# Moving the weights of a float32r kernel to other byte distances from the operands that stream past them

## The chip, the cores and the metric

The kernel runs on one core of a Trainium2 chip. The metric is the device time in microseconds (us) of one launch. Three runs of the kernel before gave 824.92, 824.91 and 824.10 us, median 824.91 us.

## The reference

One attention block feeds two feed-forward layers. All is float32, with 4 batches, 8 heads, 576 positions and head width 64.

```python
attn = softmax(mask(q @ k.T / 8)) @ v        # mask: blocks of 64 positions, block-causal
x = attn.transpose(0, 2, 1, 3).reshape(2304, 512)
h = x @ w_in                                 # 512 -> 2048
g = max(h, 0) + log1p(exp(-abs(h)))
x = g @ w_out                                # 2048 -> 512
h = x @ w_in2                                # 512 -> 1024
s = h * softmax(h)                           # over the 1024
ln = (s - mean(s)) / sqrt(var(s) + 1e-6) * g_ln
out = ln @ w_out2                            # 1024 -> 512
```

## The kernel before

**Numbers in two parts.** The feed-forward products are made from float32r operands. Every operand is split in a high part (a float32r copy) and a low part (the rest), and a product is three matmuls: high by high, high by low and low by high. So each product's stationary operand (128 x 128, called the weights below) is loaded for every matmul, and 256 or 512 columns of the moving operand stream past it.

**Layer 1** runs over 9 chunks of 256 tokens (`NCH`, `CT`), and in each over 8 pairs of blocks of 128 features (`Pair`, line 572). `Pair.a` (line 614) makes one block's `h` in 12 matmuls into the PSUM tile `hp`: weights `w1t[f]`, moving `xt` (the attention's output, high and low). ACT and DVE make `g` and split it into `gh` and `gl` (lines 623 to 642). `Pair.b` (line 647) adds the block to the output in 12 matmuls into `acc` (or `R` for chunk 1): weights `w2t[f]`, moving `gh` or `gl`. Chunks leave through DRAM (`x2s`). There are 1728 matmuls of 256 columns in `a` and 1728 in `b`.

**Layer 2** runs over 18 groups of 128 tokens (`Tok`, line 780). `Tok.a` (line 829): 24 matmuls of 512 columns into `h`; the weights are the tokens (`xh` and `xl`, which lie in `w1t[4]` and `w1t[5]`), the moving operand is `u1`. DVE and ACT make the softmax and the normalised rows `e`, PE transposes them (`tr`, line 891, float32, through `ident`) into `tp`, ACT and DVE split them into `lh` (line 900) and `ll` (line 905). `Tok.bm` (line 910): 24 matmuls of 512 columns into `op`; the weights are `lh` and `ll`, the moving operand is the second weight matrix, which lies in `w1t[6]` to `w1t[13]`. The last group makes its 24 as 48 of 256 columns.

**Where the tiles lie.** A pool's tiles stand one behind the other in each SBUF partition, in the order of their first use, with sizes rounded to 32 bytes. On the left stand the pools `w` (w1_4 to w1_15, w2_0 to w2_15, ident, gcol), `l1` (t, gh, gl, stg with 2 buffers each of 2048 bytes; 21 small tiles of 32 bytes), `xt` (3 buffers of 8192 bytes) and `wx` (w1_0 to w1_3), whose room `p2` (xr, e, ob of layer 2) takes later. On the right, against the upper end, stand the attention's pools and later `u1`. The program of the kernel before has these start addresses in bytes:

| tile | start | used as |
|---|---|---|
| w1_4 ... w1_15 | 16512 + 4096 each | weights of `Pair.a`; tokens, second matrix and `lh` in layer 2 |
| w2_0 ... w2_15 | 65664 + 4096 each | weights of `Pair.b` |
| ident | 131200 | moving operand of the transposes |
| gh, gl | 135840, 137888, 139936, 141984 | moving operand of `Pair.b` |
| xt | 148800, 156992, 165184 | moving operand of `Pair.a`; the first also `ll` in layer 2 |
| w1_0 ... w1_3 | 173376 + 4096 each | weights of `Pair.a` |
| e0, e1 | 177472, 181568 | weights of the transposes of layer 2 |
| u1 | 190432, 206816 | moving operand of `Tok.a` |

Inside a tile all steps between the blocks that one matmul reads are multiples of 512 bytes, so the distance "start of the weights minus start of the moving operand", taken modulo 512, is the same for all matmuls of one kind.

**Order.** All tasks are listed with dependencies, durations and ranks; a planner (`Plan.run`, line 89) puts them in an order once, while the program is built, and engines run their queues in that order. Waits between engines come from the tiles' regions that instructions read and write. `ln_hi` before waits for the last use of `w1t[14]` or `w1t[15]` (`w1_free`, line 763), and `t_q` (line 778), which opens the PSUM pool of `tp` and `op`, for the last matmul of layer 1, for the last readers of the first `xt` buffer, and for the last attention parts.

Of the kernel before, what the change touches and what calls it, by code (L numbers as in the profile page):

```python
# [10 lines left out]
F32 = mybir.dt.float32  # L11
F32R = mybir.dt.float32r
# [26 lines left out]
NCH = NT // CT  # L39
# [12 lines left out]
class Plan:  # L52
# [8 lines left out]
    def add(self, eng, dur, rank, fn, deps=(), lat=None):  # L61
        t = _Task()
        t.key = key_of(fn)

        t.alts = dict(eng) if isinstance(eng, dict) else {eng: dur}
        name, i = t.group = self.group
        t.local = rank
        t.rank = rank + RANK[name][0] + RANK[name][1] * i + OFF.get(t.key, 0.0) + OFF.get(t.key + "@" + name, 0.0)
        t.eng, t.fn, t.n, t.done = None if len(t.alts) > 1 else eng, fn, len(self.tasks), False
        t.lat = (self.LAT + (120.0 if eng == "PE" else 0.0)) if lat is None else lat  # L70
        t.users, t.left, t.ready = [], 0, 0.0
        for d in deps:
            if d is not None:
                d.users.append(t)
                t.left += 1
        self.tasks.append(t)
        return t
# [5 lines left out]
    def chain(self, eng, rank, steps, deps):  # L83
        for dur, fn in steps:
            t = self.add(dur if isinstance(dur, dict) else eng, dur, rank, fn, deps)
            deps = [t]
        return t
# [83 lines left out]
def key_of(fn):  # L171
    while isinstance(fn, partial):
        fn = fn.func
    return ".".join(fn.__qualname__.split(".")[-2:])


def act_ns(n):
    return 70.0 + 0.833 * n


def dve_ns(n, per=1.04):
    return 70.0 + per * n
# [6 lines left out]
def dma_ns(nbytes, n=1):  # L189
    return max(50.0 + nbytes / 360.0, 550.0 * n)  # L190
# [3 lines left out]
def body(ctx: ExitStack, tc: tile.TileContext, qk, qkA, vP, vA, w1, w2, u1, u2, gln, out):  # L194
    nc = tc.nc
    PE, ACT, DVE, POOL, SP = nc.tensor, nc.scalar, nc.vector, nc.gpsimd, nc.sync
    plan = Plan()
    XTB, LAG = 3, 2
    add, chain = plan.add, plan.chain
# [13 lines left out]
    def at_of(lst, i):  # L213
        return lst[i] if 0 <= i < len(lst) else None
# [4 lines left out]
    def pool(name, side, **kw):  # L219
        return tc.tile_pool(name=name, bufs=1, side=side, reuse_waits="tile", **kw)  # L220
# [3 lines left out]
    pw = left.enter_context(pool("w", "left"))  # L224
    pl1 = left.enter_context(pool("l1", "left"))
    pxt = left.enter_context(pool("xt", "left"))
# [3 lines left out]
    state = {}  # L230


    w1t = [(px if f < 4 else pw).tile([128, 2, 512], F32R, name=f"w1_{f}") for f in range(16)]
    w2t = [pw.tile([128, 2, 512], F32R, name=f"w2_{f}") for f in range(16)]
    ident = pw.tile([128, 128], F32, name="ident")
    gcol = pw.tile([128, 8], F32, name="gcol")
    acc = qsh.tile([128, 2, 512], F32, name="acc")
    hps = [qsh.tile([128, 2, CT], F32, name=f"hp{i}") for i in range(2)]

# [58 lines left out]
    xt = {}  # L298

    def xt_of(c):  # L300
        if c not in xt:
            xt[c] = pxt.tile([128, 2, 4, CT], F32R, tag="xt", name="xt", bufs=XTB)
        return xt[c]


# [6 lines left out]
    def xfree(c):  # L312

        return [t for u in pairs if u.c == c - XTB for t in (u.t_a0, u.t_a1)]
# [255 lines left out]
    xparts = {}  # L570
# [94 lines left out]
    stored, evacs = {}, {}  # L665
# [27 lines left out]
    def open_u():  # L693
        right[0].close()
        right[0] = ExitStack()
        pu1 = right[0].enter_context(pool("u1", "right"))
        state["qh2"] = right[0].enter_context(pool("qh2", "right", space=PSUM))
        state["u1"] = [pu1.tile([128, 4, DF2], F32R, name=f"u1{i}") for i in range(2)]
        state["cv"] = [(pu1.tile([128, 512, 2], I32, name="raw_u"), pu1.tile([128, 512], I32, name="a_u"))]
        SP.dma_start(out=gcol, in_=gln)  # L700

    def open_2():
# [10 lines left out]
    def open_q():  # L713
        psl.close()
        state["qtr"] = left.enter_context(pool("qtr", "left", space=PSUM))
        state["ll"] = xt_of(NCH).rearrange("p a b c -> p (a b c)")

    NR, NCA = 3, 4
    t_open = add("POOL", 500, 0.0, open_a, ())
# [1 line left out]
    pairs, unitsA, unitsC = [], [], []  # L721
# [9 lines left out]
    def w_of(t, i):  # L731
        return lambda: t[:, i]
# [7 lines left out]
    for kind, f in todo:  # L740
        src, t, done = (w1[f], w1t[f], w1ready) if kind == "w1" else (w2[f * 128:f * 128 + 128, :], w2t[f], w2ready)
        p = Piece(src, w_of(t, 0), w_of(t, 1))
# [8 lines left out]
    t_b = add("DVE", 200, 0, open_b, [u.t_xl for u in unitsA] + [x for p in pieces for x in (p.t_lo, p.t_hi)] + evacs[1])  # L751
# [5 lines left out]
    t_u = add("SP", 1, 0, open_u, [x for u in unitsC for x in u.t_x])  # L757
    upieces, u1d, u2d = [], [], []

    def u1_of(i, f):  # L760
        return lambda: state["u1"][i][:, :, f * 128:f * 128 + 128]

    def w1_free(f):
        return [(pairs[8 * (NCH - 1) + f // 2].t_a0, pairs[8 * (NCH - 1) + f // 2].t_a1)[f % 2]]

    for f in range(8):
        p = Piece(u1[f], u1_of(0, f), u1_of(1, f))
# [4 lines left out]
    for f in range(8):  # L772
        p = Piece(u2[f * 128:f * 128 + 128, :], w_of(w1t[6 + f], 0), w_of(w1t[6 + f], 1), gcol[:, f:f + 1])
# [1 line left out]
        plan.at_group("U2", f)  # L775
        p.plan(upieces, 0.0, conv_u, 3 if f > 2 else n + 1, 3 if f > 2 else n + 1, [t_u, t_2], w1_free(6 + f))
        u2d.append(p.t_lo)
    t_q = add("PE", 1, 0, open_q, evacs[NCH - 1] + [pairs[-1].t_b1, t_u] + xfree(NCH) + xparts[NCH - 1])

    class Tok:  # L780
        def __init__(self, t):
# [2 lines left out]
        def plan(self, prev):  # L784
            t = self.t
            rank = 0.0
            plan.at_group("Tok", t)
            p1, p2, p3 = (at_of(prev, len(prev) - k) for k in (1, 2, 3))
            o1 = (lambda *names: [getattr(p1, x) for x in names] if p1 else [])
            o2 = (lambda *names: [getattr(p2, x) for x in names] if p2 else [])  # L790
            o3 = (lambda *names: [getattr(p3, x) for x in names] if p3 else [])
            self.t_load = add("SP", dma_ns(262144), rank - 4, self.load,
                              [t_2] + stored[t // 2] + o2("t_xl", "t_xh") + o1("t_load"), DMA_LAT)
            self.t_xh = add({"ACT": 520, "DVE": 335}, None, rank, self.x_hi, [self.t_load] + o2("t_a") + (w1_free(4 + t) if t < 2 else []))
            self.t_xl = add("DVE", 610, rank, self.x_lo, [self.t_xh])
            self.t_a = add("PE", 5600, rank + 1.9, self.a, [self.t_xl] + u1d + o2("t_u") + o1("t_a"))
            t_m = add("DVE", dve_ns(1024), rank, self.max, [self.t_a])
            t_e = add("ACT", 1090, rank, self.exp, [t_m] + o2("t_tr") + ([x.t_bits for x in upieces[-3:]] if t < 2 else []))
            self.t_u = add("DVE", dve_ns(1024), rank, self.mul, [t_e])
            t_c = chain("DVE", rank, ((600, partial(self.stats, 0)), (600, partial(self.stats, 1)), (110, self.aggr),  # L800
                                      (600, self.center)), [self.t_u])
            t_s = chain("DVE", rank, [(75, partial(self.small1, i)) for i in range(4)], [t_c])
            t_s = add("ACT", 335, rank, self.logexp, [t_s])
            self.t_s = chain("DVE", rank, [(75, partial(self.small2, i)) for i in range(3)], [t_s] + o3("t_ob"))
            self.t_tr = add("PE", 870, rank + .5, self.tr, [t_c, t_q] + o1("t_ll", "t_tr"))
            self.t_lh = add("ACT", 2 * act_ns(512), rank, self.ln_hi, [self.t_tr] + o2("t_b") + (w1_free(14 + t) if t < 2 else []))
            self.t_ll = add("DVE", 2 * dve_ns(512), rank, self.ln_lo, [self.t_lh] + [t_q])

            w = DM // 2 if t == NT // 128 - 1 else DM
            for c in range(0, DM, w):  # L810
                cols = slice(c, c + w)
                self.t_b = add("PE", 5600 * w / DM, rank + 1, partial(self.bm, cols), [self.t_ll] + u2d + o2("t_ob") + (o1("t_b") if c == 0 else [self.t_b] + o1("t_ob")))
                self.t_ob = add("ACT", act_ns(w) + 90, rank, partial(self.o_evac, cols), [self.t_b, self.t_s] + o2("t_st"))
                self.t_st = add("SP", dma_ns(512 * w), rank, partial(self.store, cols), [self.t_ob], DMA_LAT)
            prev.append(self)
# [82 lines left out]
                self.tp.append(tp)  # L898

        def ln_hi(self):  # L900
            self.lh = w1t[14 + self.t % 2].rearrange("p a (k t) -> p (a k) t", k=4)
            for g in range(2):
                ACT.activation(self.lh[:, 4 * g:4 * g + 4, :], self.tp[g], AF.Copy)

        def ln_lo(self):
            self.ll = state["ll"][:, 1024 * (self.t % 2):1024 * (self.t % 2) + 1024].rearrange("p (k t) -> p k t", k=8)
            for g in range(2):
                DVE.tensor_sub(self.ll[:, 4 * g:4 * g + 4, :], self.tp[g], self.lh[:, 4 * g:4 * g + 4, :])

# [91 lines left out]
```

## Time and profile before

| | |
|---|---|
| median of 3 runs | 824.91 us |
| the profiled execution's own time | 823.77 us |
| its span, first to last instruction | 822.0 us |
| granted TensorE clock, mean | 0.996 |
| PE, DVE, ACT busy | 97%, 66%, 48% |

The profile is one execution, so 1.77 us of its time lie around the span, and it is 1.14 us under the median. Matmuls are pipelined: a matmul's record is longer than its turn on the array, and records overlap. What a matmul costs in a full stream is the distance from its start to the next one's start, called the pitch here; it is read from the starts in the timeline, not from the mean durations.

### The profile page before, as it was taken

Reading aid. Unit: us, or ns where it says so; the run is one execution under the profiler, and the core shown is the slowest. Engines: PE = TensorE matmul, PEld = TensorE weight load, DVE = VectorE, ACT = ScalarE, POOL = GpSimd, SP = SyncE. Lnnn points to the kernel's source line nnn. Section 1 sums busy time; section 2 is a strip of 40 time slices with the busy share of each in tenths; the row PEclk is TensorE's granted clock in tenths of the full one; section 3 lists DMA queues with packets and bytes.
Section 4 is the critical chain, followed back from the end, with each engine's and each line's share of the span. In section 5 each row is a group of like instructions: output and inputs, shape, how many; then the busy total and the mean of one; then the engine's idle time right before and its main releaser. Section 6 shows DMA issues by size and latency. Waiting matters only on the chain.

```text
span 822.0 us, 14229 instructions
## 1 busy us (share of the span) xinstructions
PE 798.6 (97%) x5656; PEld 689.0 (84%) x5656; DVE 546.3 (66%) x1273; ACT 391.9 (48%) x863; POOL 0.7 (0%) x6
## 2 busy tenths in 40 slices
PE   6689999999999999999999999999999999999998
PEld 4478999999888888888888889999998888888887
DVE  6999999565565656655556653777949486766661
ACT  5666765554555555455454543646623232322232
POOL 0000000000000000000000000000000000000000
PEclk9899999999999999999999999999999999999999
DMA  5544451202121112112111100326301111110001
GB/s 180 198 159 156 167 177 56 83 31 75 48 66 41 41 41 66 41 55 77 41 41 56 44 1 26 104 83 201 116 27 52 50 36 45 52 38 27 26 26 51
DMA packets 31201, 59.63 MB, mean 73 GB/s; under 512 B 2848, under 2 KB 14368, under 8 KB 31136
## 3 DMA queue, kind: packets, MB, share of 16 engines
q1 hardware_dynamic: 31136, 58.74, 22.1%
q8 instruction: 44, 0.72, 0.4%
q14 instruction: 21, 0.17, 0.1%
HBM read 49.29 MB, written 9.44 MB: 71 GB/s over the span
## 4 chain that ended last, share of the span: by engine, by line
PE 86%; DVE 7%; DMA 3%; ACT 2%; issue 1%; SPq 0%; ACTq 0%; DVEq 0%
PE hp L203 21%; PE acc L203 21%; PE h L203 12%; PE op L203 12%; PE S L203 6%; PE O L203 5%; PE T L430 4%; DMA raw<-in_w_dram 3%; PE R L203 2%; PE tp L897 2%; DVE a L278 1%; PE r L203 1%; DVE a L274 1%; DVE mA L521 1%; DVE w L288 1%
## 5 line engine op out<-in xcount | busy, mean ns | idle before, releaser
L203 PE MATMUL hp<-xt,w 128*128 128x256 f32 x1728 | 220.1, 282 | 1.5 <-DVE t L634 1.5
L203 PEld LDWEIGHTS hp<-xt,w 128*128 128x128 f32 x1728 | 207.3, 189 | 5.5 <-issue 3.4
L203 PE MATMUL acc<-gh,w 128*128 128x256 f32 x1024 | 203.2, 287 | 0.0
L203 PEld LDWEIGHTS acc<-gh,w 128*128 128x128 f32 x1024 | 163.1, 188 | 18.8 <-issue 18.4
L203 PE MATMUL acc<-gl,w 128*128 128x256 f32 x512 | 143.4, 280 | 1.1 <-DVE gl L642 1.1
L203 PE MATMUL h<-u,w 128*128 128x512 f32 x432 | 103.5, 396 | 0.0
L203 PEld LDWEIGHTS acc<-gl,w 128*128 128x128 f32 x512 | 96.4, 188 | 1.7 <-DVE gl L642 1.7
L203 PEld LDWEIGHTS h<-u,w 128*128 128x128 f32 x432 | 80.7, 188 | 19.1
L203 PE MATMUL op<-w,w 128*128 128x512 f32 (+1 forms) x304 | 91.6, 385 | 0.0
L625 ACT ACTIVATE t<-hp 128x512 f32<-128x512 f32 x72 | 42.9, 596 | 82.8 <-PE hp L203 77.8
L209 ACT ACTIVATE ps<-T 128x512 f32<-128x512 f32 (+1 forms) x77 | 42.7, 555 | 77.1 <-PE T L430 62.3
L634 DVE SCALAR_TENSOR_TENSOR t<-hp,t 128x512 f32<-128x512 f32 x72 | 49.4, 686 | 28.7 <-ACT t L631 28.2
L203 PEld LDWEIGHTS op<-w,w 128*128 128x128 f32 x304 | 55.0, 188 | 10.6
L203 PE MATMUL op<-w,xt 128*128 128x512 f32 (+1 forms) x152 | 58.0, 382 | 0.0
L409 ACT ACTIVATE eC<-S,mC 128x384 f32<-128x384 f32 (+2 forms) x80 | 51.8, 654 | 11.5 <-DVE mC L403 11.4
L399 DVE TENSOR_REDUCE mC<-S 128x2 f32<-128x768 f32 (+2 forms) x48 | 46.9, 976 | 8.5 <-PE S L203 7.8
L203 PE MATMUL S<-qkC 64*128 64x384 f32 (+2 forms) x192 | 51.9, 532 | 0.0
L642 DVE TENSOR_TENSOR gl<-t,gh 128x512 fp32r<-128x512 f32 x72 | 49.6, 689 | 2.8 <-ACT gh L209 1.5
L849 ACT ACTIVATE e<-h,mx 128x1024 f32<-128x1024 f32 x18 | 20.1, 1117 | 56.6 <-PE tp L897 50.3
L631 ACT ACTIVATE t<-t 128x512 f32<-128x512 f32 x72 | 45.4, 631 | 2.0
L628 ACT ACTIVATE t<-t 128x512 f32<-128x512 f32 x72 | 45.4, 631 | 1.1
L430 PE MATMUL T<-ident,eC 128*128 128x128 f32 x288 | 44.7, 273 | 0.0
(141 smaller groups left out, 976.1 us busy)
## 6 DMA issues: line engine op xcount, KB each, us to landing
raw<-in_w_dram SPq DMA_DIRECT2D x32, 512.0 KB, 4.0
qkC<-in_qk_dram SPq DMA_DIRECT2D x16, 480.0 KB, 3.4
raw_u<-in_u_dram SPq DMA_DIRECT2D x11, 512.0 KB, 3.5
v<-in_vP_dram SPq DMA_DIRECT2D x16, 320.0 KB, 3.0
x2s<-stg SPq DMA_DIRECT2D x18, 256.0 KB, 2.2
xr<-x2s SPq DMA_DIRECT2D x18, 256.0 KB, 3.2
qkA<-in_qkA_dram SPq DMA_DIRECT2D x16, 256.0 KB, 3.3
out_dram<-ob SPq DMA_DIRECT2D x15, 256.0 KB, 2.0
```

The costliest lines, as they stand in the source:

```text
L203: PE.matmul(out, lhsT, rhs, start=start, stop=stop, skip_group_check=True)
L209: ACT.activation(out, a, AF.Copy)
L399: DVE.tensor_reduce(out=self.m[:, 0:n], in_=self.scores(i), axis=AX.X, op=ALU.max, negate=True)
L409: ACT.activation(state["eC"][i][:, j, :], self.scores(i)[:, j, :], AF.Exp, scale=0.125, bias=m[:, j:j + 1], accum_out=den[:, j:j + 1])
L430: PE.transpose(T[:, 128 * k:128 * k + 128], e[:, 128 * k:128 * k + 128], ident)
L625: ACT.activation(self.t, self.hp, AF.Abs)
L628: ACT.activation(self.t, self.t, AF.Exp, scale=-1.0)
L631: ACT.activation(self.t, self.t, AF.Ln, bias=1.0)
L634: DVE.scalar_tensor_tensor(out=self.t, in0=self.hp, scalar=0.0, in1=self.t, op0=ALU.max, op1=ALU.add)
L642: DVE.tensor_sub(self.gl, self.t, self.gh)
L849: ACT.activation(self.e, self.hh, AF.Exp, bias=self.mx, accum_out=self.ss)
L897: PE.transpose(tp[:, k, :], self.e[:, f * 128:f * 128 + 128], ident)
```

## The change

Tiles get other start addresses; no instruction is added to or taken from an engine's arithmetic. `w2_12` to `w2_15` become slices of two wide tiles, of which the first has 64 unused elements more. `lh` and `ll` move from `w1t[14]`, `w1t[15]` and the first `xt` buffer into these two tiles, and the dependencies that guarded the old rooms go. `gcol` grows, and three tiles that nothing reads or writes (`pad_x`, `pad_u`, `pad_l`) shift what stands behind them.

```diff
-    w2t = [pw.tile([128, 2, 512], F32R, name=f"w2_{f}") for f in range(16)]
+    w2t = [pw.tile([128, 2, 512], F32R, name=f"w2_{f}") for f in range(12)]
+    wide = [pw.tile([128, 2048 + 64 * (1 - i)], F32R, name=f"w2w_{i}") for i in range(2)]
+    w2t += [t[:, 1024 * i:1024 * i + 1024].rearrange("p (h f) -> p h f", h=2) for t in wide for i in range(2)]
+    lln, lhn = wide[0][:, 64:], wide[1]
...
-    gcol = pw.tile([128, 8], F32, name="gcol")
+    gcol = pw.tile([128, 48], F32, name="gcol")[:, 0:8]
...
             xt[c] = pxt.tile([128, 2, 4, CT], F32R, tag="xt", name="xt", bufs=XTB)
+            if len(xt) == XTB:
+                pxt.tile([128, 16], F32, name="pad_x")
...
+        pu1.tile([128, 24], F32, name="pad_u")
...
-        state["ll"] = xt_of(NCH).rearrange("p a b c -> p (a b c)")
+        pl1.tile([128, 24], F32, name="pad_l")
...
-    t_q = add("PE", 1, 0, open_q, evacs[NCH - 1] + [pairs[-1].t_b1, t_u] + xfree(NCH) + xparts[NCH - 1])
+    t_q = add("PE", 1, 0, open_q, evacs[NCH - 1] + [pairs[-1].t_b1, t_u])
...
-            self.t_lh = add("ACT", 2 * act_ns(512), rank, self.ln_hi, [self.t_tr] + o2("t_b") + (w1_free(14 + t) if t < 2 else []))
+            self.t_lh = add("ACT", 2 * act_ns(512), rank, self.ln_hi, [self.t_tr] + o2("t_b"))
...
-            self.lh = w1t[14 + self.t % 2].rearrange("p a (k t) -> p (a k) t", k=4)
+            self.lh = lhn[:, 1024 * (self.t % 2):1024 * (self.t % 2) + 1024].rearrange("p (k t) -> p k t", k=8)
...
-            self.ll = state["ll"][:, 1024 * (self.t % 2):1024 * (self.t % 2) + 1024].rearrange("p (k t) -> p k t", k=8)
+            self.ll = lln[:, 1024 * (self.t % 2):1024 * (self.t % 2) + 1024].rearrange("p (k t) -> p k t", k=8)
```

## Rows read from the trace of the kernel before

**Rows 1.** The page: span, busy time of each engine, the chain that ended last.

```profile
span 822.0 us, 14229 instructions
PE 798.6 (97%) x5656; PEld 689.0 (84%) x5656; DVE 546.3 (66%) x1273; ACT 391.9 (48%) x863; POOL 0.7 (0%) x6
PE 86%; DVE 7%; DMA 3%; ACT 2%; issue 1%; SPq 0%; ACTq 0%; DVEq 0%
```

**Rows 2.** Windows: stretch, its length, busy us (instructions) per engine, granted clock, DMA.

```profile
20.00:60.00 40.00, 31.37 (x234) 23.94 (x233) 38.85 (x108) 25.74 (x72) 0.00 (x0) 0.91 0.54 176
60.00:100.00 40.00, 37.95 (x318) 35.52 (x318) 38.28 (x85) 27.63 (x59) 0.00 (x0) 1.00 0.53 176
...
100.00:150.00 50.00, 48.65 (x410) 46.13 (x409) 43.67 (x94) 31.37 (x69) 0.00 (x0) 1.00 0.32 105
...
433.00:510.00 77.00, 77.00 (x615) 66.68 (x614) 39.96 (x101) 35.48 (x77) 0.00 (x0) 1.00 0.09 29
510.00:606.00 96.00, 96.00 (x805) 94.91 (x804) 72.87 (x130) 53.12 (x89) 0.00 (x0) 1.00 0.33 109
680.00:788.00 108.00, 108.00 (x506) 88.59 (x505) 69.44 (x150) 29.45 (x63) 0.00 (x0) 1.00 0.11 35
```

**Rows 3.** Timeline of PE: start us, length us, line, matmul out<-moving,weights, shape, count.

```profile
510.33 5.91 PE L203 MATMUL hp<-xt,w 128*128 128x256 f32 x48
516.07 0.28 PE L203 MATMUL acc<-gh,w 128*128 128x256 f32 x1
...
517.48 2.90 PE L203 MATMUL hp<-xt,w 128*128 128x256 f32 x24
520.21 0.28 PE L203 MATMUL acc<-gh,w 128*128 128x256 f32 x1
...
521.61 2.90 PE L203 MATMUL hp<-xt,w 128*128 128x256 f32 x24
```

**Rows 4.** Groups of PE by shape, 100:822 us, then 0:100: count, busy us, mean ns.

```profile
L203 PE MATMUL hp<-xt,w 128*128 128x256 f32 x1512 | 192.6, 281 | 0.0
L203 PE MATMUL acc<-gh,w 128*128 128x256 f32 x960 | 190.6, 287 | 0.0
L203 PE MATMUL acc<-gl,w 128*128 128x256 f32 x480 | 134.3, 280 | 0.5 <-DVE gl L642 0.5
L203 PE MATMUL h<-u,w 128*128 128x512 f32 x432 | 103.5, 396 | 0.0
L203 PE MATMUL op<-w,w 128*128 128x512 f32 x272 | 85.9, 397 | 0.0
L203 PE MATMUL op<-w,xt 128*128 128x512 f32 x136 | 53.6, 394 | 0.0
...
L203 PE MATMUL R<-gh,w 128*128 128x256 f32 x44 | 8.5, 282 | 0.0
L203 PE MATMUL R<-gl,w 128*128 128x256 f32 x22 | 6.2, 280 | 0.0
```

**Rows 5.** Timeline of PE, layer 2: one block of `h`, blocks of `op`, transposes.

```profile
644.14 0.63 PE L203 MATMUL op<-w,w 128*128 128x512 f32 x2
...
655.24 1.04 PE L897 MATMUL tp<-ident,e 128*128 128x128 f32 x8
...
676.71 0.61 PE L203 MATMUL op<-w,w 128*128 128x512 f32 x2
...
678.10 0.63 PE L203 MATMUL op<-w,w 128*128 128x512 f32 x2
...
680.17 5.75 PE L203 MATMUL h<-u,w 128*128 128x512 f32 x24
685.76 1.03 PE L897 MATMUL tp<-ident,e 128*128 128x128 f32 x8
```

**Rows 6.** Timeline of PE, the last group: `op` in matmuls of 256 columns.

```profile
812.96 0.39 PE L203 MATMUL op<-w,w 128*128 128x256 f32 x2
813.19 0.28 PE L203 MATMUL op<-w,xt 128*128 128x256 f32 x1
813.31 0.40 PE L203 MATMUL op<-w,w 128*128 128x256 f32 x2
...
818.49 0.28 PE L203 MATMUL op<-w,xt 128*128 128x256 f32 x1
```

**Rows 7.** Timeline of PE in the attention's stretch: transposes beside layer 1.

```profile
356.72 3.12 PE L203 MATMUL hp<-xt,w 128*128 128x256 f32 x24
359.68 0.60 PE L430 MATMUL T<-ident,eC 128*128 128x128 f32 x4
...
375.89 3.00 PE L203 MATMUL hp<-xt,w 128*128 128x256 f32 x24
```

**Rows 8.** The tile tp: the transposes of layer 2, first and last start.

```profile
L897 PE MATMUL tp<-ident,e x144: 270/272/273, 613.5 to 807.3; 128*128 128x128 f32 x144
```

**Rows 9.** Timeline of DVE: `ll` written while other tokens' `ll` is in use.

```profile
680.26 1.28 DVE L908 TENSOR_TENSOR xt<-tp,w 128x512 fp32r<-128x512 f32 x2
692.27 1.28 DVE L908 TENSOR_TENSOR xt<-tp,w 128x512 fp32r<-128x512 f32 x2
```

## Prediction, before the result was known

> **What bounds the kernel now.** I read the page first. PE is busy for 97% of the span and holds 86% of the chain that ended last [rows 1]. The windows then show where that is so: from 20 to 100 us DVE is busy for 38.9 and 38.3 us of each 40 and PE has gaps, so DVE sets the pace there; from 100 us on PE is busy for 48.7 of 50 us and soon for every microsecond of each stretch, at a granted clock of 1.00, while DVE has a quarter or more of its time free [rows 2]. So from 100 us on a nanosecond less per matmul is a nanosecond less in the run, as often as it occurs, and before 100 us it is worth nothing.
>
> Busy time can't tell whether a matmul is as short as it can be, because records overlap. The starts can. In the timeline of layer 1, away from the attention, 48 matmuls of `Pair.a` start at 510.33 and the next kind at 516.07: 5.74 us / 48 = 119.6 ns each. These four blocks have weights w1_0 to w1_3. The next 24, with w1_4 and w1_5, run from 517.48 to 520.21: 2.73 / 24 = 113.8 ns. Twelve of `Pair.b` run from 520.21 to 521.61: 1.40 / 12 = 116.7 ns [rows 3]. It is the same shape, 128 x 128 weights and 256 columns, on the same engine at the same clock, in three pitches. The first two even do the same job with the same `xt`; what differs is where the weights lie.
>
> From the address table (distance is weights minus moving, modulo 256): w1_0 to w1_3 against xt, 173376 - 148800, is 0. w1_4 and later against xt, 16512 - 148800, is 64. w2 against gh, 65664 - 135840, is 224, that is 32 on the other side. So 0 gives 119.6, 32 gives 116.7, 64 gives 113.8: each 32 bytes farther apart takes off 2.9 ns. The last group's `op` in 256 columns is a check from another stage: there `lh` is at distance 0 twice and `ll` at 192 (64 on the other side) once, which by this line would be (2 x 119.6 + 113.8) / 3 = 117.7; measured, 47 pitches from 812.96 to 818.49 us are 5.53 / 47 = 117.7 ns [rows 6]. In the attention's stretch the first kind is longer by as much: 24 matmuls of w1_0 and w1_1 take 3.12 us, 24 of w1_4 and w1_5 3.00 [rows 7].
>
> The Trainium skill speaks against this. Its page "SBUF — State Buffer", section "SBUF: two separate sides", gives TensorE two independent read ports, one for the moving operand and one for the weight load, and says that PE never waits on anyone; by that the places of the operands can't matter and the change is worth 0 us. The rows disagree for these shapes: 119.6, 116.7 and 113.8 ns.
>
> **The change, part by part.** First the new distances. The wide tiles add 256 bytes and gcol 160, so `l1` starts 416 later: w2 against gh and gl becomes -32 - 416 = -448, which is 64 (modulo 256). w2_14 and w2_15 lie 256 further, still 64. pad_l makes `xt` start 512 later: w1_4 and later stay at 64. pad_x puts w1_0 to w1_3 64 further against xt: 64 instead of 0. `u1` on the right starts 96 lower; the tokens in w1_4 and w1_5 against it are now at 160 modulo 512 (16512 - 190432), then at 256. `lh` goes from 0 and `ll` from 192 (148800 against w1_6 and later) to 256 modulo 512, both. So the code does give the distances that it names.
>
> 1. `Pair.b`, 32 to 64: after 100 us there are 960 + 480 matmuls into acc, and 192 - 66 = 126 into R [rows 4], together 1566, by 116.7 - 113.8 = 2.9 ns: 4.5 us.
>
> 2. `Pair.a` with w1_0 to w1_3, 0 to 64: chunks 2 to 8 lie after 100 us, 7 x 4 x 12 = 336 matmuls by 119.6 - 113.8 = 5.8 ns: 1.9 us. The other `a` matmuls keep their 113.8.
>
> 3. `Tok.a`, 160 to 256, and `Tok.bm`, 0 and 192 to 256, both of 512 columns. A block of `h` takes 680.17 to 685.76, 5.59 / 24 = 232.9 ns; two blocks of `op` 644.14 to 655.24, 11.10 / 48 = 231.3 ns [rows 5]. No row shows 512 columns at 256. Distances as unlike as 160 and 0 or 192 lie within 2 ns here, so the line of the 256 columns doesn't carry over. Bounds: inside `op` two matmuls in a row take 0.61 to 0.63 us, which with 0.39 for the last is a pitch between 0.22 and 0.24 us [rows 5]. I take 220 as the low end and 240 as the high end, which is also about twice 119.6. The value I take is 227.6, twice the best pitch of 256 columns: `h` 432 x 5.3 = 2.3 us, `op` 408 x 3.7 = 1.5 us, together 3.8. At 220 it is 5.6 + 4.6 = 10.2 us; at 240 it is a loss of 3.1 + 3.5 = 6.6 us.
>
> 4. Small things. 48 matmuls of the last group go from a mean of 117.7 to distance 0 modulo 256, 119.6: 0.1 us lost. The transposes' weights `e` against `ident` go from 192 to 0 (modulo 256): 144 of them; the pitch is (1.03 - 0.27) / 7 = 109 ns at 192 and (0.60 - 0.27) / 3 = 110 in the attention at another distance [rows 5, 7, 8], so I take no cost; at the 5.8 ns of step 2 it would be 0.8 us.
>
> 5. The waits that go. `t_q` follows the last matmul of layer 1 anyway, which comes after the last readers of the old rooms; the first transposes start at 613.5 us [rows 8], when layer 1 is over (606 us, the last window's edge in which it runs). So the removed dependencies were never last, and 0 is gained. The planner knows durations, not pitches, and no task's readiness changes, so I expect the same order on each engine. No wait is added: `lh` and `ll` of two tokens share a tile each, but waits go by regions, as those of `ll` do now: its halves are written every 12 us, each once [rows 9], and PE has no gap there [rows 2].
>
> Sum: 4.5 + 1.9 + 3.8 - 0.1 = 10.1 us. Against the profiled execution, 823.77 - 10.1 = 813.7 us. That execution stood 1.14 us under the median of 824.91, so the median to expect is 814.8. What is late next: PE still; over a group's 12 us DVE is busy for 64% and ACT for 27% (69.44 and 29.45 of 108 us) [rows 2], and PE would be quicker by only 2%. Layer 1 without attention is tightest, DVE at 72.87 of 96 us.
>
> **The rivals.** (a) Only the 256 columns gain; 512 columns don't care, as 160, 0 and 192 lie so close together already. Then 4.5 + 1.9 - 0.1 = 6.3 us, 818.6. (b) The 512 columns gain fully, pitch 220: 16.5 us, 808.4. For it: single pitches of 0.22 exist. Against: no block has that mean. (c) The distance isn't the cause and the blocks w1_0 to w1_3 and `Pair.b` differ by something else, so nothing changes, or the change of pitch is made up by a later wait for DVE: 824.9. Against: three stages fall on one line. This is also what the Trainium skill's rule of the two ports (page "SBUF — State Buffer", above) would give. (d) Slower: 256 modulo 512 is the bad place for 512 columns, as 0 is for 256, with the weight load meeting the stream in each half: two penalties of 5.8 ns per half on 227.6 give 250.8 ns, a loss of 432 x 17.9 + 408 x 19.5 = 15.7 us against 6.3 gained, 834.3. It decides from a pitch of about 240 on, the longest that rows show; nothing shows a mean above 233.
>
> **How the numbers follow.** Forecast 0.55, (a) 0.22, (b) 0.12, (c) 0.06, (d) 0.05. What tells a change from none is about 0.2%, 1.65 us. The forecast, (a) and (b) are faster by more: 0.89. (c) is the same, 0.06, and (d) slower, 0.05. The range goes from (b) to a little past (a): 808 to 820 us.
>
> **What would show it.** Pitches in the timeline of the new kernel: `Pair.b` 113.8 ns, w1_0 to w1_3 113.8, w1_4 and later unchanged, `h` and `op` at the same pitch of some 228 with a group's period of 12.0 us [rows 9] cut to 11.8; the order of PE's work unchanged; DVE's idle time larger. I am wrong in the mechanism if `Pair.b` stays at 116.7, and in a size if `h` and `op` lie elsewhere.

## The result, and the profile after

The changed kernel took 818.17 us (median of 6 runs, 815.35 to 819.75) against 824.91 us before (6 runs, 822.11 to 826.65): ratio 0.9918, 95% interval [0.9894, 0.9942]. Two later comparisons on other occasions gave 0.9889 [0.9874, 0.9904] and 0.9885 [0.9858, 0.9913] (experiments 9 and 12). So the change is faster by 7 to 9 us; the forecast was 10.1. The time by itself can't tell the forecast from its rival (a): 818.17 us lies nearer to the 818.6 of (a) than to 814.8. The pitches below do.

| | before | after |
|---|---|---|
| the profiled execution's own time | 823.77 us | 818.25 us |
| its span | 822.0 us | 816.5 us |
| granted TensorE clock, mean | 0.996 | 0.991 |

The page after, span, busy time and chain, against [rows 1]:

```profile
span 816.5 us, 14229 instructions
PE 790.5 (97%) x5656; PEld 684.6 (84%) x5656; DVE 546.0 (67%) x1273; ACT 391.9 (48%) x863; POOL 0.7 (0%) x6
PE 80%; DVE 13%; DMA 3%; ACT 2%; issue 2%; SPq 0%; ACTq 0%; DVEq 0%
```

PE's busy time fell by 8.1 us, the span by only 5.5, and DVE's share of the chain rose from 7 to 13%. The order of PE's 5656 matmuls is the same in both, so the pitches can be compared one by one. The timeline of PE in layer 1, away from the attention, against [rows 3]:

```profile
508.30 5.60 PE L203 MATMUL hp<-xt,w 128*128 128x256 f32 x48
513.74 0.28 PE L203 MATMUL acc<-gh,w2w 128*128 128x256 f32 x1
...
515.10 2.88 PE L203 MATMUL hp<-xt,w 128*128 128x256 f32 x24
517.82 0.28 PE L203 MATMUL acc<-gh,w2w 128*128 128x256 f32 x1
...
519.17 2.88 PE L203 MATMUL hp<-xt,w 128*128 128x256 f32 x24
```

The blocks of w1_0 to w1_3 take 5.44 / 48 = 113.3 ns (119.6 before), those of w1_4 and w1_5 2.72 / 24 = 113.3 (113.8), `Pair.b` from 517.82 to 519.17 1.35 / 12 = 112.5 from the timeline's two digits, and 113.4 over all such blocks from 510 to 576 us (116.7): one pitch for all three. Layer 2, against [rows 5]:

```profile
641.35 11.05 PE L203 MATMUL op<-w,w2w 128*128 128x512 f32 x48
652.24 1.04 PE L905 MATMUL tp<-ident,e 128*128 128x128 f32 x8
...
676.74 5.61 PE L203 MATMUL h<-u,w 128*128 128x512 f32 x24
682.18 1.03 PE L905 MATMUL tp<-ident,e 128*128 128x128 f32 x8
...
688.51 1.75 PE L203 MATMUL h<-u,w 128*128 128x512 f32 x7
```

`op` takes 10.89 / 48 = 226.9 ns (231.3), `h` 5.44 / 24 = 226.7 (232.9), and a group's period, 676.74 to 688.51, is 11.77 us (12.0). The distances did what was forecast, within a nanosecond. What is missing of the sum lies in three places. The first is the start, here the windows:

```profile
20.00:60.00 40.00, 30.34 (x212) 23.97 (x211) 37.56 (x105) 24.32 (x69) 0.00 (x0) 0.83 0.53 173
60.00:100.00 40.00, 38.35 (x327) 35.79 (x327) 38.86 (x88) 27.86 (x60) 0.00 (x0) 1.00 0.56 176
```

The granted clock from 20 to 60 us is 0.83, against 0.91 in [rows 2]: PE, which waits there for loads and for ACT and DVE (9.9 us in all, 8.5 before), ran longer at the lower of its two levels, 1.2 instead of 2.4 GHz: some 14 of the 40 us against 7. At 100 us its work was 1.3 us behind the profile of before. The second is the attention's stretch, blocks of w1_0 and w1_1 and then of w1_4 and w1_5, against [rows 7]; the third row is a block of layer 1 near its end:

```profile
356.40 3.00 PE L203 MATMUL hp<-xt,w 128*128 128x256 f32 x24
375.29 3.00 PE L203 MATMUL hp<-xt,w 128*128 128x256 f32 x24
...
579.03 2.99 PE L203 MATMUL hp<-xt,w 128*128 128x256 f32 x24
581.86 0.28 PE L203 MATMUL acc<-gh,w 128*128 128x256 f32 x1
```

24 matmuls went from 3.12 to 3.00 us, as forecast for these. But near the end the same distance has a second pitch, 2.83 / 24 = 117.9 ns: at 64, matmuls run at 113.4 or at 117.8, and beside the attention (200 to 505 us) a third of the matmuls of `Pair.b` and nearly half of those with w1_0 to w1_3 are in the slower one. The third place is the end of layer 1, PE's timeline:

```profile
598.82 0.28 PE L203 MATMUL acc<-gh,w 128*128 128x256 f32 x1
599.81 0.38 PE L203 MATMUL acc<-gh,w2w 128*128 128x256 f32 x1 [0.71 <-DVE gh L211]
600.53 0.38 PE L203 MATMUL acc<-gl,w2w 128*128 128x256 f32 x1 [0.34 <-DVE gl L649]
```

From 598.82 to 600.53 PE starts two matmuls instead of some fifteen: it waits for DVE's `gh` and `gl` of the last pair. There was no such wait in the profile of before.

### The profile page after: what moved, and what is told of

It reads as the page before. It is cut to its first block, busy times and chain, and to the rows that moved or that the text cites. A ratio compares the mean times of both kernels' runs of the same rounds, so it can differ in the third digit from the quotient of the medians.

```text
span 816.5 us, 14229 instructions
## 1 busy us (share of the span) xinstructions
PE 790.5 (97%) x5656; PEld 684.6 (84%) x5656; DVE 546.0 (67%) x1273; ACT 391.9 (48%) x863; POOL 0.7 (0%) x6
## 4 chain that ended last, share of the span: by engine, by line
PE 80%; DVE 13%; DMA 3%; ACT 2%; issue 2%; SPq 0%; ACTq 0%; DVEq 0%
PE hp L203 19%; PE acc L203 18%; PE op L203 12%; PE h L203 11%; PE S L203 6%; PE O L203 5%; PE T L437 4%; PE tp L905 2%; PE R L203 2%; DVE a L283 2%; DMA raw<-in_w_dram 2%; DVE a L279 1%; DVE t L641 1%; DVE gl L649 1%; PE r L203 1%
## 5 line engine op out<-in xcount | busy, mean ns | idle before, releaser
L203 PE MATMUL acc<-gh,w 128*128 128x256 f32 x768 | 150.3, 286 | 0.0
L203 PEld LDWEIGHTS acc<-gh,w 128*128 128x128 f32 x768 | 122.4, 189 | 13.0 <-issue 12.5
L203 PE MATMUL acc<-gl,w 128*128 128x256 f32 x384 | 107.0, 279 | 0.6 <-DVE gl L649 0.6
L203 PE MATMUL op<-w,w2w 128*128 128x512 f32 (+1 forms) x456 | 102.3, 381 | 0.0
L203 PE MATMUL h<-u,w 128*128 128x512 f32 x432 | 100.9, 390 | 0.0
L203 PEld LDWEIGHTS op<-w,w2w 128*128 128x128 f32 x456 | 81.5, 188 | 15.3
L203 PEld LDWEIGHTS acc<-gl,w 128*128 128x128 f32 x384 | 72.7, 189 | 0.8 <-DVE gl L649 0.8
L203 PE MATMUL acc<-gh,w2w 128*128 128x256 f32 x256 | 50.2, 285 | 0.9 <-DVE gh L211 0.7
L203 PEld LDWEIGHTS acc<-gh,w2w 128*128 128x128 f32 x256 | 40.5, 188 | 6.9 <-issue 5.5
```

The source lines that it names most:

```text
L203: PE.matmul(out, lhsT, rhs, start=start, stop=stop, skip_group_check=True)
```

## The experiments

**1 and 2: each half of the change alone.** Experiment 1 moves only what layer 2 reads:

```diff
-    gcol = pw.tile([128, 48], F32, name="gcol")[:, 0:8]
+    gcol = pw.tile([128, 8], F32, name="gcol")
...
-            if len(xt) == XTB:
-                pxt.tile([128, 16], F32, name="pad_x")
...
-        pl1.tile([128, 24], F32, name="pad_l")
```

> The changed kernel with gcol, pad_l and pad_x as before: the 512-column matmuls of layer 2 at distance 256, the 256-column ones at their old 32 and 0. If the distance alone sets the pitch: h and op at 227 ns, Pair.b at 116.7, Pair.a with w1_0 to w1_3 at 119.6, and a time 3.8 us under before (ratio 0.9954), with no wait of PE at the end of layer 1 and the granted clock of the start as in the kernel before (0.996 over the span). Rival, the gain of layer 2 is given back by a wait on DVE in it: h and op at 227 but the group's period still 12.0 us, ratio 1.000.

Measured 821.95 us, ratio 0.9965 [0.9949, 0.9982], 2.9 us. `h` in the timeline:

```profile
680.61 5.61 PE L203 MATMUL h<-u,w 128*128 128x512 f32 x24
686.05 1.03 PE L902 MATMUL tp<-ident,e 128*128 128x128 f32 x8
```

5.44 / 24 = 226.7 ns, and `Pair.b` stays at 117. The forecast holds for the pitches, and the 3.8 us lie inside the interval. Against the expectation, PE in this kernel too waits at the end of layer 1 (it loses 1.3 us over three places) and has a mean clock of 0.992, though its layer 1 is no quicker than before.

Experiment 2 takes the other half, in the kernel before:

```diff
-    gcol = pw.tile([128, 8], F32, name="gcol")
+    gcol = pw.tile([128, 48], F32, name="gcol")[:, 0:8]
...
+            if len(xt) == XTB:
+                pxt.tile([128, 16], F32, name="pad_x")
...
+        pl1.tile([128, 24], F32, name="pad_l")
```

> The kernel before with gcol, pad_l and pad_x of the change: only the 256-column matmuls move, to distance 64; lh, ll and u1 stay. If the distance sets the pitch: Pair.a and Pair.b at 113.4 ns, h and op as before (231 to 233). My theory on the missing 3.4 us: the quicker layer 1 runs into DVE at its end (a wait of some 1.9 us before the last pair's Pair.b) and its start spends more time at the half clock (about 1.8 us), so 6.4 - 3.7 = 2.7 us faster (ratio 0.9967). Rival, these two belong to the moved lh and ll or to chance: 6.4 us faster (ratio 0.9922), clock 0.996 over the span, no wait at the end of layer 1.

Measured 821.27 us, ratio 0.9961 [0.9946, 0.9977], 3.2 us, with all of layer 1 at 113.4 ns where nothing disturbs it and `h` still at 5.59 / 24 = 232.9. The two halves add up to 6.1 us, which is the whole change within the intervals; the 256-column half is the one that falls short of its 6.3. As expected, PE waits at the end of layer 1 here; it loses 2.0 us there.

**3: farther.** All matmuls of layer 1 at distance 128:

```diff
-    gcol = pw.tile([128, 48], F32, name="gcol")[:, 0:8]
+    gcol = pw.tile([128, 32], F32, name="gcol")[:, 0:8]
...
-                pxt.tile([128, 16], F32, name="pad_x")
+                pxt.tile([128, 32], F32, name="pad_x")
```

> The changed kernel with gcol of 32 elements and pad_x of 32: all 256-column matmuls of layer 1 at distance 128 (modulo 256) instead of 64, layer 2 as in the change. Theory of a floor (64 is already far enough): pitch 113.4 and the time of the changed kernel, within 1 us. Rival line: 2.9 ns less for each further 32 bytes, pitch 107.7 and some 17 us less. Rival period of 128 bytes: 128 is as bad as 0, pitch 119.6 and some 15 us more than the changed kernel.

Measured 825.89 us, ratio 1.0013 [0.9997, 1.0028], some 8 us over the changed kernel:

```profile
516.70 5.86 PE L203 MATMUL hp<-xt,w 128*128 128x256 f32 x48
522.39 0.28 PE L203 MATMUL acc<-gh,w2w 128*128 128x256 f32 x1
...
523.82 3.01 PE L203 MATMUL hp<-xt,w 128*128 128x256 f32 x24
526.66 0.28 PE L203 MATMUL acc<-gh,w2w 128*128 128x256 f32 x1
```

5.69 / 48 = 118.5 ns and 2.84 / 24 = 118.3, for every block, also for w1_4 and w1_5, which have the same weights in the same place as ever. So the line of 2.9 ns per 32 bytes turns round past 64. The pitch is near the 119.6 ns of the rival of a period of 128 bytes; experiment 6 speaks against that period. The time is less bad than that rival's 15 us, since beside the attention the changed kernel doesn't keep its 113.4 ns either: from 100 to 505 us the mean pitch, without the gaps of 200 ns and more, is 114.9 ns there and 118.8 here.

**4: a planner that knows the new durations.** 1450 to 1365 ns in four places, 5600 to 5450 in two:

```diff
-            self.t_a0 = add("PE", 1450, rank, partial(self.a, 0), wd + xd + o("t_stt") + one("t_a1"))
+            self.t_a0 = add("PE", 1365, rank, partial(self.a, 0), wd + xd + o("t_stt") + one("t_a1"))
...
```

> The changed kernel with the planner told the new lengths of PE's tasks: 1365 ns instead of 1450 for the twelve matmuls of Pair.a and Pair.b, 5450 instead of 5600 for Tok.a and Tok.bm; the order of the work is planned anew. If the lost time at the end of layer 1 is an order that suits the old pace, the wait of 1.9 us before the last Pair.b goes, 816.3 us or a ratio to before of 0.9895. Rival: the ranks suit the old durations and the new order is no better or worse, 818 us and up (ratio 0.992 or more).

Measured 826.37 us, ratio 1.0025 [1.0007, 1.0044]: the rival. The new order differs from the start on; PE now waits for ACT and DVE (after 100 us 2.4 us for `psA`, 1.7 for `t`, 0.9 for `ps`, 8.2 in all), and the 8 us are gone. Why the order from the true lengths is the worse one isn't shown; that the ranks suit the old durations is the rival's guess.

**5 and 6: other distances for 512 columns.** Layer 2 at 0 and at 64, starting from experiment 1:

```diff
-    wide = [pw.tile([128, 2048 + 64 * (1 - i)], F32R, name=f"w2w_{i}") for i in range(2)]
-    lln, lhn = wide[0][:, 64:], wide[1]
+    wide = [pw.tile([128, 2048], F32R, name=f"w2w_{i}") for i in range(2)]
+    lln, lhn = wide
...
-        pu1.tile([128, 24], F32, name="pad_u")
+        pu1.tile([128, 88], F32, name="pad_u")
```

> As e1_wide_only, but all 512-column matmuls at distance 0 (modulo 512) instead of 256: the two wide tiles without the 64 unused elements, pad_u of 88 elements; layer 1 at its old distances. Theory of a period of 128 bytes with the phases turned round for 512 columns (0 good, 32 middle, 64 bad): h and op at 227 ns, as at 256. Rival, a period of 512 with 256 as the far end and 0 as the worst: 235 to 241 ns.

Measured 821.29 us (one run), `h`:

```profile
679.81 5.61 PE L203 MATMUL h<-u,w 128*128 128x512 f32 x24
685.25 1.03 PE L902 MATMUL tp<-ident,e 128*128 128x128 f32 x8
```

226.7 ns: 0 is as good as 256 for 512 columns, while it is the worst place for 256 columns.

```diff
-    wide = [pw.tile([128, 2048 + 64 * (1 - i)], F32R, name=f"w2w_{i}") for i in range(2)]
-    lln, lhn = wide[0][:, 64:], wide[1]
+    wide = [pw.tile([128, 2048 + 16 * (1 - i)], F32R, name=f"w2w_{i}") for i in range(2)]
+    lln, lhn = wide[0][:, 16:], wide[1]
...
-        pu1.tile([128, 24], F32, name="pad_u")
+        pu1.tile([128, 104], F32, name="pad_u")
```

> As e1_wide_only, but all 512-column matmuls at distance 64 (modulo 512): 16 unused elements instead of 64, pad_u of 104. The shift also puts all of Pair.a at distance 0 and Pair.b at 160 (32 modulo 128). Theory of the period of 128: h and op at 239 to 240 ns, all blocks of Pair.a at 120, those with w1_4 and later too, Pair.b at 116.7. Rival, 64 is good for 512 columns as for 256: 227 ns. Rival on layer 1, the blocks and not the distance: w1_4 and later stay at 113.4.

Measured 834.80 us (one run):

```profile
517.34 5.91 PE L203 MATMUL hp<-xt,w 128*128 128x256 f32 x48
524.50 3.03 PE L203 MATMUL hp<-xt,w 128*128 128x256 f32 x24
...
531.64 0.28 PE L203 MATMUL acc<-gh,w 128*128 128x256 f32 x1
...
534.52 3.04 PE L203 MATMUL hp<-xt,w 128*128 128x256 f32 x24
...
690.50 5.76 PE L203 MATMUL h<-u,w 128*128 128x512 f32 x24
696.10 1.03 PE L902 MATMUL tp<-ident,e 128*128 128x128 f32 x8
```

Layer 1 settles the main question: blocks with w1_4 and w1_5, 2.90 us long in [rows 3], now take 3.03 like those of w1_0 to w1_3. It is the distance and not the block. The last group's `op` in 256 columns, far from layer 1, goes the same way: 117.7 ns in the kernel before, 119.8 in the changed kernel (distance 0), 113.4 here (distance 64). `Pair.b` missed what was expected of it: with w2_0 to w2_13, at 160, two blocks take 2.88 / 24 = 120.0 ns (119.6 on the mean from 515 to 576 us) and not 116.7; only w2_14 and w2_15, which stay at 224, have 116.8. So a period of 128 bytes is refuted for 256 columns as well. `h` takes 5.60 / 24 = 233.3 ns: 64 is worse than 0 for 512 columns, but no worse than 160 (232.9). The 239 to 240 that I expected from a period of 128 are not there.

**7: the kernel before again,** unchanged.

> The kernel before, unchanged. What it tells is the scatter: its granted clock and its wait at the end of layer 1 in further executions. If the lost time of the change (1.8 us at the half clock in the first 60 us, 1.8 us of waiting before the last Pair.b) is of every execution and the profile of before was a lucky one, this shows a clock of 0.985 to 0.993 in most runs and the wait of 1 to 2 us. Rival, the change brings both: clock 0.996 in all runs and no wait. Ratio 1.000.

Measured 825.13 us (12 runs), ratio 1.0002 [0.9987, 1.0018]. Its windows:

```profile
20.00:60.00 40.00, 30.90 (x215) 24.02 (x216) 37.32 (x105) 24.03 (x69) 0.00 (x0) 0.83 0.50 166
60.00:100.00 40.00, 38.62 (x325) 36.30 (x324) 38.79 (x87) 27.50 (x59) 0.00 (x0) 1.00 0.56 176
```

The clock of the start is 0.83 here too, and over the 12 runs the mean clock goes from 0.986 to 0.998, with times from 827.6 down to 822.9. So the lower clock at the start belongs to both kernels and goes with much of the scatter; as to the clock, the first profile of before was a lucky one. The theory of experiment 2, that the quicker layer 1 brings the lower clock, fell. As to the wait, this profile has one of 0.22 us and not of 1 to 2.

**8, 10 and 11: ACT's queue at the end of layer 1.** The changed kernel with one number:

```diff
-            self.t_load = add("SP", dma_ns(524288), rank, self.load, dep, DMA_LAT)
+            self.t_load = add("SP", dma_ns(524288), rank, self.load, dep, DMA_LAT if self.g is None else 5500.0)
```

What it is about stands in ACT's timeline of the changed kernel:

```profile
565.61 0.60 ACT L632 ACTIVATE t<-hp 128x512 f32<-128x512 f32 x1 [0.51 <-PE hp L203]
569.08 0.66 ACT L273 ACTIVATE ob<-e 128x512 f32<-128x512 f32 x1 [2.87 <-DMA e<-in_u_dram]
569.65 0.67 ACT L273 ACTIVATE a_u<-raw_u 128x512 f32<-128x512 f32 x1
570.22 0.62 ACT L635 ACTIVATE t<-t 128x512 f32<-128x512 f32 x1
```

The first activation of a pair is done at 566.2; the second (line 635) stands in the queue behind a step on the second matrix, whose load lands at 569.0, and starts at 570.22. The chain of waits of the changed kernel names this load as one of its longest pieces:

```profile
562.50 6.56 DMA e<-in_u_dram
```

> The changed kernel with one planner number: the loads of the second matrix of layer 2 count as landing after 5.5 us instead of 1.7, so that ACT's first step on them is queued behind the activations of the last pairs. If the lost 1.8 us at the end of layer 1 is ACT held up in its queue by a load that lands 6.5 us after its issue, PE's wait before the last Pair.b goes and the time is 816.4 us (ratio to before 0.990 or less). Rival, DVE's work in that stretch (19.8 of 20 us busy) is the bound: the wait stays or moves, 818 us (0.992).

Measured 816.36 us (5 runs), ratio 0.9889 [0.9872, 0.9906]. Between 540 and 650 us PE has no wait for another engine any more. ACT in this kernel:

```profile
568.95 0.60 ACT L632 ACTIVATE t<-hp 128x512 f32<-128x512 f32 x1 [3.12 <-PE hp L203]
569.58 0.63 ACT L635 ACTIVATE t<-t 128x512 f32<-128x512 f32 x1
570.12 0.65 ACT L273 ACTIVATE a_u<-raw_u 128x512 f32<-128x512 f32 x1
```

The pair goes first, and the load's step waits for nothing. But the number moves more than this step. PE's first block of `h`, which lies inside the end of layer 1, now comes 14 blocks later, four operations go from ACT to DVE, from 590 to 600 us DVE is busy for 7.0 us instead of 8.7, and fewer matmuls of layer 1 follow that block at the second pitch (48 at 117.8 ns, against 95 to 168 in the three profiles of the changed kernel). So the run shows that another order takes the wait away, and not which of its moves does.

What ties PE's wait to the load are the profiles that keep the order. These rows are ACT's waits for such loads from 555 to 585 us, with the longest as the last number, in the kernel before, in experiments 12, 7 and 9, and in the first profile of the changed kernel:

```profile
ACT ob L268 <- DMA e<-in_u_dram: 1.6, 2, 1.1
ACT ob L273 <- DMA e<-in_u_dram: 2.0, 3, 1.5
ACT ob L268 <- DMA e<-in_u_dram: 2.1, 2, 1.6
ACT ob L273 <- DMA e<-in_u_dram: 3.1, 3, 2.3
ACT ob L273 <- DMA e<-in_u_dram: 3.2, 2, 2.9
```

At the end of layer 1 PE loses 0, 0.3, 0.5, 1.1 and 2.0 us in them (what the distances between starts over 150 ns have above a pitch), and experiments 1 and 2 fit in with 2.5 and 1.3, 2.6 and 2.0: the longer ACT is held, the more PE loses. Two things make up the holding. With the quicker layer 1 (the changed kernel and experiment 2) the first activation is done 3.7 to 3.8 us after the load's issue, with the old pitches (before, experiments 1, 5 and 7) 4.4 to 4.7 us after it: this part, 0.6 to 1.0 us, comes with the change. And from the load's issue to ACT's step on it 6.6, 6.0 and 5.2 us pass in the three profiles of the changed kernel: this part differs between executions of one kernel.

> The kernel before with the one planner number of e8_late_abs and the old distances. If the end of layer 1 gave back time only because the change makes PE arrive there earlier, the number is worth little here: about 0.5 us, the wait of e7_before_again, ratio 0.9994. Rival, the new order is worth its 2 us with any distances: ratio 0.9976, and the two edits simply add.

The same number in the kernel before: 824.72 us (12 runs), ratio 0.9983 [0.9968, 0.9998], 1.4 us: between both theories, with an interval that holds both. It moves PE's block of `h` in the same way, and from 576 us to the end of layer 1 it takes as long as the first profile of before, 31.6 us.

> e8_late_abs again, beside the changed kernel on one chip. If its gain at the end of layer 1 is real, it is 0.7 to 1.8 us under the changed kernel (e10_before_late_abs gained 0.7 to 1.4 over before), ratio to before 0.988 to 0.989. Rival: no difference, both at 0.990.

Measured 815.61 us (6 runs), ratio 0.9870 [0.9846, 0.9894]. Both times it has the lowest median of all kernels here. That it beats the kernel before is clear; that it beats the changed kernel isn't shown by the times (next paragraphs).

**9 and 12: the changed kernel again.**

> The changed kernel, unchanged, for a direct comparison on one chip and for a second profile. If the wait before the last Pair.b is of every execution of it: again 1.5 to 2 us there, and a ratio to before of 0.992. Rival, it was chance in the first profile: no wait there and 0.990.

Measured 817.50 us (4 runs), ratio 0.9889 [0.9874, 0.9904], and PE's waits between 540 and 650 us:

```profile
PE acc L203 <- DVE gl L649: 0.3, 1, 0.3
PE acc L203 <- DVE gh L211: 0.2, 1, 0.2
```

> The changed kernel, for the comparison with e11_late_abs_again: between its two earlier ratios, 0.990, and a wait before the last Pair.b of 1 to 2 us.

Measured 817.46 us (6 runs), ratio 0.9885 [0.9858, 0.9913], and no wait in that stretch. So the expected waits of 1.5 to 2 and of 1 to 2 us did not come, and the wait is not of every execution: it is 1.05, 0.5 and 0 us as the trace counts it, and goes with the landing of one load. Beside experiment 11 on the same chip the changed kernel is 1.85 us slower by the medians (817.46 against 815.61), with intervals that overlap.

## Why the prediction was right, and where its sum was too large

**The mechanism** was right. Where nothing disturbs the stream, distances set the pitch, in all three kinds of matmuls, and the rivals are refuted by experiments 6 (c, the block and not the distance) and 1 (d, 256 as the bad place; a, no gain in 512 columns; b, a pitch of 220). Where the Trainium skill's page "SBUF — State Buffer", section "SBUF: two separate sides", has PE wait for nobody with two independent read ports, the same matmuls took 113.4, 116.7, 118.6 or 119.6 ns as the distance was 64, 224, 128 or 0: the measurement decides. What in the chip makes the distance count, no run here shows.

**Step 3** came out as sized. From the first block of `h` after layer 1 to the last `op`, the changed kernel gained 3.62 us against the profile of before in each of its three profiles; the term was 3.8, the small loss in the last group 0.1. To take 227.6, twice the best 256-column pitch, was a guess between 220 and 240, without a row at distance 256; that 226.7 was measured was luck.

**Steps 1 and 2** were sized at 4.5 + 1.9 = 6.4 us. Between 100 us and the last part of layer 1 (576 us in the profile of before) the three profiles of the changed kernel gained 5.0, 5.1 and 5.2 us against the first profile of before, and 0.5 less against the second (experiment 7). Away from the attention the terms were even small: 3.3 and 6.3 ns instead of 2.9 and 5.8. In the attention's stretch, from 200 to 505 us, `Pair.b` gained 2.3 ns on the mean (125.3 to 123.0, the long gaps after transposes included) and the blocks of w1_0 to w1_3 3.4 (123.4 to 120.0), since part of them runs at 117.8. The trace of before had this second pitch already, in blocks of w1_4 and later beside the attention; the prediction read the undisturbed rows and applied them to all.

**The step that failed** is the first one: "from 100 us on a nanosecond less per matmul is a nanosecond less in the run". It holds until some 576 us. In the last 30 us of layer 1 the changed kernel lost again 1.8, 1.2 and 0.4 us in the three profiles, the kernel before 0 and 0.5 in its two. The waits there cost 2.0, 1.1 and 0.3 us. The second pitch comes on top: right after the block of `h` in that stretch, 95, 167 and 168 matmuls of layer 1 run at 117.8 ns and not at 113.4, which is 0.4, 0.7 and 0.7 us. What the other matmuls gain there stands against both.

I looked at DVE's free time, and at that wrongly, and not at what stands in ACT's queue in front of the pairs: a step that waits for a load. From 100 to 150 us DVE is busy for 43.67 of 50 us [rows 2], so an eighth is free and not a quarter; and the mean from 510 to 606 us hides stretches without room. The first row is of the kernel before, the others of the changed kernel:

```profile
580.00:590.00 10.00, 10.00 (x76) 9.41 (x75) 9.89 (x18) 6.19 (x11) 0.00 (x0) 1.00 0.34 113
570.00:580.00 10.00, 10.00 (x66) 9.05 (x66) 9.86 (x19) 7.52 (x13) 0.00 (x0) 1.00 0.61 210
580.00:590.00 10.00, 10.00 (x88) 10.00 (x87) 9.89 (x18) 6.40 (x11) 0.00 (x0) 1.00 0.27 80
```

DVE is the third engine of a row, after PE and its weight loads, and busy for 9.86 to 9.89 of ten microseconds. So what ACT holds up there DVE can't make up for; how much less PE would lose with a freer DVE wasn't tested.

I also named "the order of PE's work unchanged" and "the removed dependencies were never last", and both held: the 5656 matmuls have the same order, and `lh` waits for nothing new.

**The sum** with what was measured: 4.8 + 3.6 - (1.1 - 0.3) = 7.6 us, from the means of the three profiles after and the two before. By the ratios the first comparison has 6.8 and the later ones 9.2 and 9.5 us. The start's clock, which experiment 2 took for a loss by the change, belongs to both.

## What to carry to other kernels

When weights are loaded for every matmul, read the pitch from the starts of the matmuls, kind by kind, and set it beside the tiles' addresses; two kinds of the same shape with unlike pitches are a free experiment. A few unused bytes in front of a tile are a cheap edit, but a distance that is good for 256 columns can be bad for 512, so each shape has to be measured. And before PE is made faster in a stretch, look for in-order queues of other engines in which a step that waits for a load stands before what PE needs.

## What the runs showed of the hardware

The mean pitch of float32r matmuls with 128 x 128 weights loaded each time, at full clock, undisturbed, by the distance of the weights from the moving operand:

| distance | 256 columns (modulo 256) | 512 columns (modulo 512) |
|---|---|---|
| 0 | 119.6 to 120 ns | 227 ns |
| 64 | 113.4 ns, at times 117.8 | 233.3 ns |
| 128 | 118.6 ns | |
| 160 | 119.6 ns | 233 ns |
| 224 (32 on the other side) | 116.7 ns | |
| 256 | | 227 ns |

The entries for 512 columns at 0 and at 64 and for 256 columns at 160 rest on one run each (experiments 5 and 6).

I had not expected that 0 and 64 change places between the two lengths, nor a second pitch at the best distance. What decides between the two pitches at 64 the traces show for one place, the blocks right after the first block of `h`. Where `h` is at 160 (both profiles of before, experiment 2), blocks at 64 follow at 113.3 to 113.7 ns; where it is at 256 or 0 (the three profiles of the changed kernel, experiments 1, 5, 8 and 11), they follow at 117.8, with the same tiles. In the changed kernel the 117.8 hold over both kinds of blocks until PE's stream breaks at a wait; after it come 113.4. So there the stream keeps the pitch with which it was entered. Why, and why there are two, stays open.
